# Placing the last two casts and transposes earlier in the list of a fused retention and mixer kernel

## The chip, the cores and the metric

The kernel runs on one core of one Trainium2 chip. The metric is the device time of one execution in microseconds (us). The time before is 333.81 us, the median of three runs (332.57, 333.81 and 334.24). The traced execution is a further one: it took 332.29 us, of which 330.5 us are the span that the profile shows.

The engines are called as in the profile: PE (TensorE, its weight loads apart as PEld), DVE (VectorE), ACT (ScalarE), POOL (GpSimd) and SP (SyncE). Each works through its own list of instructions in order; a `q` behind the name (SPq) is the part that issues DMAs and waits.

## What is computed

Two stages, written as two functions in the reference. The first is a causal retention over 8 batches, 8 heads, 576 positions and a head width of 64; the second is a low-rank mixer over the positions followed by a two-layer block over the channels:

```python
scores = scale * np.matmul(q, k.transpose(0, 1, 3, 2))
Dmat = np.where(rel >= 0, gamma[:, None, None] ** rel[None, :, :], 0.0)   # rel = i - j
attn = np.matmul(scores * Dmat[None], v)
x = attn.transpose(0, 2, 1, 3).reshape(B, S, H * D)        # 8 x 576 x 512
h = x.transpose(0, 2, 1) @ U @ V                           # rank 32 over the positions
u = x + h.transpose(0, 2, 1)
out = u + np.maximum(u @ w_ch1, 0.0) @ w_ch2               # 512 -> 2048 -> 512
```

## The kernel before

**Chunks.** Batches are taken in pairs. The 2 x 576 rows of a pair are nine chunks of 128 rows: chunks 0 to 3 belong to the even batch, chunk 4 is half and half, chunks 5 to 8 belong to the odd one. Over the four pairs that makes 36 chunks, listed in `order` (L542). "Chunk (3, 8)" is chunk 8 of the last pair, pair 3.

**What a chunk needs before PE can use it.** `load` (L219) brings q, k and v as float32 from DRAM into `stage_t` tiles, with DMAs that SP issues. `prep` (L548) then does four things: `cast_qk` casts k to bfloat16 on DVE (L244) and q on ACT (L246), into one tile `qk`; `scale_v` multiplies v by its decay on POOL (L255, tile `vt`); and `xbar` issues one DMA on SP that transposes `qk` into `qkT` (L263). The transpose waits for both casts.

**What uses it.** The attention of a chunk is two items. `A(i)` (L355) runs the score matmuls `SC` on `qkT` (L276) and the matmuls `QS` of q with the running state (L301, which reads `s_sb`), and a mask on DVE (L286). `Bf(i)` (L361) runs `RV` (L315), the scaling `XS` on DVE (L326), and for all but the last chunk of a batch the state update `ST` (L341) with its copy to `s_sb` on ACT (L349). `SJ` is the state update of chunk 4. After a batch's chunks come the mixer items: `MA` (L395), then `MH` and `MT` (L422, L428, L439), which end in the transposed `uT` that the channel block of that batch reads.

**The main work.** The channel block of a batch is 16 `Y1` items (L481, evicted by ACT with a ReLU into `y`, L486) and then 16 `Y2` items of four matmuls each for a batch with four chunks (L515; the sum with u on DVE, L504; the store, L507). Its PSUM tiles come from a pool of three (`ps_big`).

**How the order is made.** The order of instructions is the order of the Python calls. From batch 2 on there is one stretch for each batch b (L1021 to L1030): the main list is the channel block of b, the list `fill` is the attention and the mixer of batch b + 1, and the list `aux` holds preps and loads for chunks later still. `merge` (L16) walks the main list and, before each main item, calls whatever of the other lists has come due. Item k of a list of n falls due at

```python
queues.append([((k + 0.5) / n * lead * total, fn) for k, fn in enumerate(fill)])
```

of the main list's nominal cost, `total`. So `lead` is the share of the stretch at which a list ends: 0.82 for `fill`, 0.58 for `aux`. Where two items fall due before the same main item, `fill` goes first.

**The stretch of batch 6.** Its main list is 32 items of nominal cost 864, total 27648. Its `fill` is `SJ` and the items `A` and `Bf` of chunks 5 to 8 of the last pair, then the mixer: 13 in all. Its `aux` is short: `aux_items` gives a prep for the chunk two places back of each g, and a load only where g is below 36; for batch 6 g runs from 36 to 39, so the list holds two preps, those of chunks (3, 7) and (3, 8), and no loads. For batch 7, g runs from 40 to 44 and the list is empty. The stretches of batches 2 and 4 have the same main list and the same `fill`, with eight `aux` items each, four preps and four loads.

Of the kernel before, what the change touches and what calls it, by code (L numbers as in the profile page):

```python
# [15 lines left out]
def merge(main, *fills, leads=(0.82, 0.64)):  # L16

    total = sum(c for c, _ in main)
    queues = []
    for fill, lead in zip(fills, leads):  # L20
        n = len(fill)
        queues.append([((k + 0.5) / n * lead * total, fn) for k, fn in enumerate(fill)])
    done = 0.0
    for cost, fn in main:
        for q in queues:
            while q and q[0][0] <= done:
                q.pop(0)[1]()
        fn()
        done += cost
    for q in queues:  # L30
        for _, fn in q:
            fn()
# [3 lines left out]
def kernel(  # L36
# [13 lines left out]
    B, H, S, D = q.shape  # L50
# [301 lines left out]
    def attn_items(pr, par):  # L352
        items = []

        def A(i):  # L355
            SC(pr, i)
            if i not in (0, J):
                QS(pr, i)
            mask(pr, i)

        def Bf(i):  # L361
            RV(pr, i)
            if i == J:
                QS(pr, i)
            XS(pr, i)
            if i not in (J, NI - 1):
                ST(pr, i)
                Scopy(pr, i)

        def SJ():  # L370
            ST(pr, J)
            Scopy(pr, J)

        if par == 1:
            items.append(SJ)
        for i in (range(0, J + 1) if par == 0 else range(J + 1, NI)):
            items.append(lambda i=i: A(i))
            items.append(lambda i=i: Bf(i))
        return items
# [86 lines left out]
    def y1_items(par, by_seg=False):  # L466
        nch = 4 + par
        segs = [(0, 4)] if par == 0 else [(0, 3), (3, 2)]
        if by_seg:
            segs = [(1, 4), (0, 1)]  # L470
        items, made = [], []

        def Y1(f, seg):
            if not made:
                made.append(1)
                st["y1", par] = y1_pool.tile(
                    [P, NF, nch * P], BF16, tag=f"y1{par}", name="y1")
            c0, n = segs[seg]
            ps = ps_big.tile([P, 4, P], FP32, tag="big", name="ps_y1")
            for cc in range(NCC):  # L480
                nc.tensor.matmul(  # L481
                    ps[:, 0:n, :], w1_sb[:, cc, f * P:(f + 1) * P],
                    st["uT", par][:, c0:c0 + n, cc, :],
                    start=(cc == 0), stop=(cc == NCC - 1),
                )
            nc.scalar.activation(  # L486
                out=st["y1", par][:, f, c0 * P:(c0 + n) * P],
                in_=ps[:, 0:n, :].rearrange("p s t -> p (s t)"), func=AF.Relu)

        ns = len(segs)  # L490
        for f in range(NF):
            items.append((nch * 216.0, lambda f=f: [Y1(f, g) for g in range(ns)]))
        if by_seg:
            return Y1, items
        return items

    def y2_items(pr, par):
        nch = 4 + par
        items = []

        def store(c, ps, w, last):
            n = w.stop - w.start
            o_sb = osb_pool.tile([P, dm], FP32, tag="o_sb", name="o_sb")
            nc.vector.tensor_tensor(  # L504
                out=o_sb[:, 0:n], in0=ps[:, 0:n], in1=st["u", par][:, c, w], op=ALU.add)
            r0 = pr * 2 * S + (c + (0 if par == 0 else J)) * P
            (nc.sync if last else nc.gpsimd).dma_start(  # L507
                out=out_flat[r0:r0 + P, w], in_=o_sb[:, 0:n])

        def Y2(c, f0):  # L510
            if f0 == 0:
                st["y2"] = ps_big.tile([P, 512], FP32, tag="big", name="ps_y2")
            ps = st["y2"]
            for f in range(f0, f0 + 4):
                nc.tensor.matmul(  # L515
                    ps, st["y1", par][:, f, c * P:(c + 1) * P], w2_sb[:, f, :],
                    start=(f == 0), stop=(f == NF - 1),
                )
            if f0 + 4 == NF:
                store(c, ps, slice(0, dm), pr == B // 2 - 1 and par == 1)  # L520

        def Y2_last(c, w):
            ps = ps_big.tile([P, 512], FP32, tag="big", name="ps_y2")
            n = w.stop - w.start
            for f in range(NF):
                nc.tensor.matmul(  # L526
                    ps[:, 0:n], st["y1", par][:, f, c * P:(c + 1) * P], w2_sb[:, f, w],
                    start=(f == 0), stop=(f == NF - 1),
                )
            store(c, ps, w, True)  # L530

        for c in range(nch):
            if pr == B // 2 - 1 and c == nch - 1 and par == 1:
                for w0, w1 in ((0, 256), (256, 384), (384, 512)):
                    items.append((1728.0, lambda c=c, w=slice(w0, w1): Y2_last(c, w)))
                continue
            for f0 in range(0, NF, 4):
                items.append((864.0, lambda c=c, f0=f0: Y2(c, f0)))
        return items
# [4 lines left out]
    def aux_items(lo, hi):  # L544

        items = []

        def prep(g):  # L548
            pr, i = order[g]
            cast_qk(pr, i)  # L550
            scale_v(pr, i)
            if pr > 0:
                xbar(pr, i)

        for g in range(lo, hi):
            if NI <= g - LAG < len(order):
                items.append(lambda g=g: prep(g - LAG))
            if g < len(order):
                items.append(lambda g=g: load(*order[g], (1, 0, 2)))
        return items  # L560
# [449 lines left out]
    with tc.manual_schedule():  # L1010
        early_consts()
        startup()
        y1_left = first_stretch()
        aux = aux_items(NI + 4, NI + 9)
        aux = [idle] + aux[0:2] + [idle] + aux[2:]
        merge(
            y1_left + y2_items(0, 0) + y2_items(0, 1),
            [idle] + attn_items(1, 0) + mixer_items(1, 0), aux, leads=(0.82, 0.62),
        )
        g = NI + 9  # L1020
        for b in range(2, B):  # L1021
            pr, par = divmod(b, 2)
            fill = []
            if b + 1 < B:
                fill = attn_items((b + 1) // 2, (b + 1) % 2) + mixer_items(
                    (b + 1) // 2, (b + 1) % 2)
            n = 5 if b % 2 == 1 else 4
            aux = aux_items(g, g + n)
            g += n
            merge(y1_items(par) + y2_items(pr, par), fill, aux, leads=(0.82, 0.58))  # L1030

# [1 line left out]
_INS = ['q', 'k', 'v', 'moe_U', 'moe_V', 'moe_w_ch1', 'moe_w_ch2']  # L1033
# [26 lines left out]
```

## Time and profile before

| | us |
|---|---|
| median of three runs | 333.81 |
| the profiled execution | 332.29 |
| its span | 330.5 |
| PE busy | 317.6 (96% of the span) |
| DVE busy | 136.4 (41%) |
| ACT busy | 136.9 (41%) |
| POOL busy | 77.8 (24%) |
| stretch of batch 2 (109.19 to 142.48) | 33.29 |
| stretch of batch 4 (183.01 to 216.30) | 33.29 |
| stretch of batch 6 (256.84 to 292.83) | 35.99 |

The granted TensorE clock is 1.0 throughout. A stretch is taken from its first `Y1` matmul to the first `Y1` matmul of the next batch, on the chain of work that ended last. In the timeline a row is a group of instructions of one line: start, length, engine, line, operation, tiles, count, and in brackets the idle time of the engine before it with what ended it. Lengths of PE rows are modelled and may overlap the next row by some hundredths; start times are records.

### The profile page before, as it was taken

To read this page: it belongs to the slowest core of one execution; us is meant where nothing else is said; L and a number is where in the kernel's file an instruction comes from. 1 tells how busy PE (TensorE), PEld (TensorE's weight loads), DVE (VectorE), ACT (ScalarE), POOL (GpSimd) and SP (SyncE) were. 2 spreads that over 40 slices of the span, in tenths; PEclk is the share of its full clock that TensorE was granted. 3 is DMA by queue.
4 is the path that set the end of the run, shared out by engine and by line. 5 is a ranking of instruction groups with operands and counts; after the bars stand their busy time and mean duration, and the time that the engine had idled before them with its cause. 6 is when DMAs were issued, how large, how long until landed. Compare 5 with 4: busy or idle time off the path is not lost.

```text
span 330.5 us, 7031 instructions
## 1 busy us (share of the span) xinstructions
PE 317.6 (96%) x2942; PEld 174.0 (53%) x2964; DVE 136.4 (41%) x193; ACT 136.9 (41%) x289; POOL 77.8 (24%) x112
## 2 busy tenths in 40 slices
PE   7899999999999999999999999999999996999996
PEld 2464554555444455467644454467644453467544
DVE  5383554444534254534334354534534342510022
ACT  2547656772200573057700573067700662037400
POOL 5675636022221311131121311131211300110000
DMA  7999999999999399949995499959995011330012
GB/s 210 236 226 257 231 196 191 184 171 198 239 238 193 101 226 172 217 125 170 189 251 136 110 218 181 205 135 193 196 211 158 32 34 33 102 106 2 0 70 91
DMA packets 151311, 53.17 MB, mean 161 GB/s; under 512 B 131984, under 2 KB 148752, under 8 KB 151280
## 3 DMA queue, kind: packets, MB, share of 16 engines
q1 hardware_dynamic: 144512, 40.40, 68.0%
q0 software_dynamic: 6768, 12.32, 14.9%
q8 instruction: 23, 0.38, 0.6%
q14 instruction: 8, 0.07, 0.1%
HBM read 36.85 MB, written 9.44 MB: 140 GB/s over the span
## 4 chain that ended last, share of the span: by engine, by line
PE 91%; DMA 3%; DVE 2%; issue 1%; SPq 1%; ACT 1%; POOL 0%
PE ps_y L481 38%; PE ps_y L515 37%; PE psc L276 3%; DMA stage_t<-in_q_dram 2%; PE po L315 2%; PE pss L341 2%; PE pss L691 1%; SPq L578 1%; PE ph L422 1%; PE ps_y L526 1%; PE pa L395 1%; PE po L301 1%; DMA qkT<-qk 1%; DVE xt L682 1%; PE po L665 1%
## 5 line engine op out<-in xcount | busy, mean ns | idle before, releaser
L481 PE MATMUL ps_y<-uT,w_sb 128*128 128x512 bf16 (+3 forms) x768 | 135.8, 326 | 0.4 <-DVE uT L702 0.4
L486 ACT ACTIVATE y<-ps_y 128x384 bf16<-128x384 f32 (+2 forms) x192 | 89.6, 489 | 112.2 <-PE ps_y L481 111.6
L515 PE MATMUL ps_y<-w_sb,y 128*128 128x512 bf16 x538 | 124.5, 379 | 1.5 <-issue 0.8
L481 PEld LDWEIGHTS <-w_sb 128*128 128x128 bf16 x768 | 69.2, 98 | 47.4 <-issue 1.4
L515 PEld LDWEIGHTS <-y 128*128 128x128 bf16 x560 | 52.2, 98 | 59.8
L504 DVE TENSOR_TENSOR o_sb<-ps_y,u 128x512 f32<-128x512 f32 (+2 forms) x38 | 25.2, 663 | 81.5 <-PE ps_y L515 79.3
L255 POOL TENSOR_TENSOR vt<-stage_t,vscale 128x512 bf16<-128x512 f32 (+1 forms) x29 | 30.2, 1049 | 85.2 <-DMA stage_t<-in_v_dram 74.4
L286 DVE TENSOR_TENSOR ret<-psc,tri 128x1024 bf16<-128x1024 f32 x24 | 29.4, 1224 | 44.1 <-PE psc L276 44.1
L507 POOL DMA_DIRECT2D out_dram<-o_sb x31 | 17.2, 554 | 117.5 <-DVE o_sb L504 111.7
L326 DVE TENSOR_TENSOR xt<-po,qscale 128x512 bf16<-128x512 f32 x27 | 18.6, 690 | 25.7 <-PE po L315 24.4
L428 DVE TENSOR_TENSOR u<-ph,xt 128x1024 bf16<-128x1024 f32 (+3 forms) x24 | 21.8, 951 | 11.0 <-PE ph L422 11.0
L246 ACT ACTIVATE qk<-stage_t 128x512 bf16<-128x512 f32 x27 | 16.9, 624 | 8.0 <-DMA stage_t<-in_q_dram 8.0
L401 ACT ACTIVATE a_sb<-pa 128x128 bf16<-128x128 f32 x8 | 2.2, 277 | 34.8 <-PE pa L395 34.8
L349 ACT ACTIVATE s_sb<-pss 128x512 bf16<-128x512 f32 x24 | 14.3, 596 | 4.7 <-PE pss L341 3.6
L647 DVE TENSOR_TENSOR ret<-psc,triU 128x1024 bf16<-128x1024 f32 x8 | 9.7, 1222 | 11.3 <-PE psc L639 11.3
L244 DVE CAST qk<-stage_t 128x512 bf16<-128x512 f32 x27 | 13.1, 485 | 0.9 <-DMA stage_t<-in_k_dram 0.9
L276 PE MATMUL psc<-qkT 64*128 64x128 bf16 x216 | 10.7, 219 | 2.6 <-DMA qkT<-qk 2.6
L596 POOL CAST qk<-stage_t 128x512 bf16<-128x512 f32 x16 | 9.7, 611 | 11.6 <-DMA stage_t<-in_q_dram 8.4
L276 PEld LDWEIGHTS <-qkT 64*128 64x128 bf16 x216 | 6.1, 94 | 11.8 <-issue 8.0
L315 PEld LDWEIGHTS <-ret 128*128 128x128 bf16 x216 | 9.9, 98 | 4.4
L190 PE MATMUL pw<-ident 128*128 128x512 bf16 x33 | 10.2, 448 | 1.4 <-POOL ident masks.py:199 1.4
L315 PE MATMUL po<-vt,ret 128*128 128x64 bf16 x216 | 10.7, 193 | 0.1
(110 smaller groups left out, 159.8 us busy)
## 6 DMA issues: line engine op xcount, KB each, us to landing
stage_t<-in_k_dram SPq DMA_DIRECT2D x32, 256.0 KB, 4.3
stage_t<-in_q_dram SPq DMA_DIRECT2D x32, 256.0 KB, 5.2
stage_t<-in_v_dram SPq DMA_DIRECT2D x32, 256.0 KB, 5.5
out_dram<-o_sb POOLq DMA_DIRECT2D x31, 256.0 KB, 3.4
w_sb<-in_moe_w_ch_dram POOLq DMA_DIRECT2D x4, 512.0 KB, 7.9
w_sb<-in_moe_w_ch_dram POOLq DMA_DIRECT2D x8, 256.0 KB, 9.0
stage_t<-in_k_dram SPq DMA_DIRECT2D x8, 128.0 KB, 3.7
stage_t<-in_q_dram SPq DMA_DIRECT2D x8, 128.0 KB, 4.4
```

The costliest lines, as they stand in the source:

```text
L246: nc.scalar.activation(out=t[rows, 0, :], in_=c["f", 0][rows].rearrange("p h d -> p (h d)"), func=AF.Copy)
L255: (eng or nc.gpsimd).tensor_tensor(out=c["v"][rows], in0=c["f", 2][rows], in1=vscale[rows, i, :, None].to_broadcast([n, H, D]), op=ALU.mult,)
L276: nc.tensor.matmul(psc[:, hl, hp, :], qkT[r, NHP + hp, :], qkT[r, hp, :], start=True, stop=True,)
L286: nc.vector.tensor_tensor(out=ret.rearrange("p (hp hl) i -> p hl hp i", hl=2), in0=c["psc"], in1=m[:, None, None, :].to_broadcast([P, 2, N ...
L315: nc.tensor.matmul(c["po"][:, hl, hp * D:(hp + 1) * D], c["ret"][:, h, :], c["v"][:, h, :], start=(first and hp == 0), stop=True, skip_gro ...
L326: nc.vector.tensor_tensor(out=xt[:, i, :].rearrange("p (hp hl d) -> p hl hp d", hl=2, d=D), in0=c["po"][:, :, 0:NHP * D].rearrange("p hl ( ...
L428: nc.vector.tensor_tensor(out=st["u", par][:, i0 - base:i0 - base + n, w].rearrange("p s (c d) -> p c s d", c=2), in0=ph[k][:, :, 0:n, :], ...
L481: nc.tensor.matmul(ps[:, 0:n, :], w1_sb[:, cc, f * P:(f + 1) * P], st["uT", par][:, c0:c0 + n, cc, :], start=(cc == 0), stop=(cc == NCC - 1),)
L486: nc.scalar.activation(out=st["y1", par][:, f, c0 * P:(c0 + n) * P], in_=ps[:, 0:n, :].rearrange("p s t -> p (s t)"), func=AF.Relu)
L504: nc.vector.tensor_tensor(out=o_sb[:, 0:n], in0=ps[:, 0:n], in1=st["u", par][:, c, w], op=ALU.add)
L507: (nc.sync if last else nc.gpsimd).dma_start(out=out_flat[r0:r0 + P, w], in_=o_sb[:, 0:n])
L515: nc.tensor.matmul(ps, st["y1", par][:, f, c * P:(c + 1) * P], w2_sb[:, f, :], start=(f == 0), stop=(f == NF - 1),)
```

## The change

The second lead of `merge` is 0.58 for batches 2 to 5 as before, and 0.3 for batches 6 and 7:

```diff
-            merge(y1_items(par) + y2_items(pr, par), fill, aux, leads=(0.82, 0.58))
+            merge(y1_items(par) + y2_items(pr, par), fill, aux,
+                  leads=(0.82, 0.58 if b < B - 2 else 0.3))
```

Batch 7's list is empty, so what moves is the two preps in the stretch of batch 6: each is a cast on DVE, a cast on ACT, a multiplication on POOL and a transposing DMA on SP. No instruction is added, removed or changed in shape.

## The prediction

> **What bounds the kernel now.** I read the busy shares first, then the chain that ended last, then that chain in order of time, and last the timeline of the one place where the chain leaves PE. The page's busy line:
>
> ```profile
> PE 317.6 (96%) x2942; PEld 174.0 (53%) x2964; DVE 136.4 (41%) x193; ACT 136.9 (41%) x289; POOL 77.8 (24%) x112
> ```
>
> PE is the bound, and no other engine is near it. So a moved cast or transpose can only matter through a time in which PE stands still. The chain, by engine:
>
> ```profile
> PE 91%; DMA 3%; DVE 2%; issue 1%; SPq 1%; ACT 1%; POOL 0%
> ```
>
> Of the 3% on DMA, 2% is the first load of q. The rest is one wait late in the kernel. The chain in order of time, between 256 and 280 us (start, length, what):
>
> ```profile
> 272.16 0.22 PE pss L341 x4
> 272.39 1.24 PE ps_y L481 x6
> 273.62 3.08 DMA qkT<-qk
> 276.70 0.05 issue
> 276.75 0.40 PE psc L276 x8
> ```
>
> Every earlier step there is PE; here the chain runs through a transposing DMA, and PE resumes when it lands. The timeline says which one:
>
> ```profile
> 263.32 11.54 SPq L263 DMA_TRANSPOSE qkT<-qk  x2
> ...
> 272.20 0.69 DVE L326 TENSOR_TENSOR xt<-po,qscale 128x512 bf16<-128x512 f32 x1 [0.95 <-PE po L315]
> 272.22 1.89 PE L481 MATMUL ps_y<-uT,w_sb 128*128 128x512 bf16 x8
> 272.48 0.60 ACT L349 ACTIVATE s_sb<-pss 128x512 bf16<-128x512 f32 x1
> 272.81 0.42 DVE L244 CAST qk<-stage_t 128x512 bf16<-128x512 f32 x1
> 272.98 0.62 ACT L246 ACTIVATE qk<-stage_t 128x512 bf16<-128x512 f32 x1
> ...
> 276.75 0.40 PE L276 MATMUL psc<-qkT 64*128 64x128 bf16 x8 [2.64 <-DMA qkT<-qk]
> ```
>
> This is chunk (3, 8). Its casts end at 272.98 + 0.62 = 273.60, the transpose starts at 273.62 and its landing frees the score matmuls at 276.75. PE had finished the matmuls before them at 272.22 + 1.89 = 274.11. It is PE's only wait for a transpose in the trace. Last, busy time by stretch, of batch 4 and of batch 6:
>
> ```profile
> 183.01:216.30 33.29, 33.02 (x283) 16.01 (x284) 15.11 (x20) 13.61 (x25) 6.33 (x8) 1.00 0.94 179
> 256.84:292.83 35.99, 33.09 (x283) 16.00 (x284) 14.11 (x18) 12.65 (x23) 4.25 (x6) 1.00 0.26 63
> ```
>
> The columns are the stretch, its length, busy time and count of PE, PEld, DVE, ACT and POOL, the granted clock, the DMA share and GB/s. Both have the same PE work (283 records, 284 weight loads), yet the second is 2.70 us longer, though its DMA engines are busy 26% of the time instead of 94%.
>
> **The change part by part.** *Where the two preps go.* An item of cost 864 in a total of 27648. Before, they fell due at 0.25 x 0.58 = 0.145 and 0.435 of it, 4009 and 12026, so before main items 5 and 14 (counted from 0). After: 0.075 and 0.225, 2074 and 6221, so before items 3 and 8. The score matmuls of chunk (3, 7) fall due at 5.5/13 x 0.82 (item 12), those of chunk (3, 8) at 7.5/13 x 0.82 (item 16). The margin ahead of the latter grows from 2 main items to 8; ahead of the former from 7 to 9.
>
> *The stall that goes.* Where no transpose is late, the start of eight Y1 matmuls and that of the score matmuls behind them lie 267.76 to 269.58 = 1.82 us apart (chunk 7 of this stretch). For chunk (3, 8) they lie 272.22 to 276.75 = 4.53 apart: 2.71 too much. The stretches say the same, 35.99 - 33.29 = 2.70. That is the term: -2.70 us, if the transpose lands before 272.22 + 1.82 = 274.04.
>
> *When it lands now.* On DVE the cast of k moves ahead of xt of chunk 6, the mask and xt of chunk 7, to just behind the mask of chunk 6. That mask runs 265.56 to 266.78, the cast 0.42, to 267.20. On ACT the cast of q moves ahead of six evictions and two copies to s_sb, to behind the eviction that starts at 265.22: it runs 265.82 to 266.44. So SP issues at about 267.2. The landing time at the new place is not in the trace; the bounds are 3.1 us (both transposes of this stretch) and 12.5 us (the longest of all 27, before 110 us, where nearly all DMA slices are full). I take 3.1, the row nearest in place and load: 270.3, 3.7 us ahead of need. Even 4.5, the longest in the stretch of batch 5, with loads beside it, leaves 2.3.
>
> *What the moved casts cost.* DVE, chunk 8: the cast fits the 0.95 us that DVE idles before xt of chunk 6 (267.74). Without that cover xt would start at most 0.42 late. DVE, chunk 7: the cast moves ahead of the mask of chunk 5, into an idle time of 3.53 us before 261.10. It waits only for loads: SP issued the last at 242.66 and landings in that window took at most 6.1 us, so all are in by about 250. Behind it wait the mask and then PE's matmuls on `ret`; a cast there could be felt only if it ended after 261.10. ACT, chunk 8: 0.62 us into the 0.82 idle before the eviction at 266.64. ACT, chunk 7: two evictions earlier, directly behind the one that ends at 260.50; it delays the next by 261.12 - 260.76 = 0.36, to an end at 261.72. With three PSUM tiles, PE writes that tile again from 263.30, so 1.6 us of cover remain. From both sides: 0 to +0.62 us, a whole cast, should that cover fail; I take 0. POOL and SP: the two multiplications and two transposes keep their places in those lists, with nothing between to be moved past; POOL has already run ahead of PE and done both by 260.47. PE's list is the same, instruction for instruction. What leaves the old places (casts at 272.81 and 272.98) was cover for nothing else.
>
> [...] The trace has three casts of k that ran beside POOL's multiplication, and they took longer: at 194.52, 232.68 and 238.03 us, 0.75, 0.72 and 1.13 us instead of 0.42, each ending 0.3 us after POOL's. The moved cast of chunk 7 goes to about 257.56, next to POOL's pair (258.42 to 260.47). [...]
>
> *What is late next.* At 274.04 the score matmuls need the PSUM tile that the mask of chunk 7 frees (270.02 + 1.23 = 271.25), and the matmuls behind them need xt of chunk 7 done (272.89) and s_sb (272.48 + 0.60 = 273.08). The latest clears with about 1 us, and ACT has one cast less before it. After the score matmuls all work follows PE, so it shifts by the same amount; the stretch of batch 4 runs through the same order with no wait.
>
> *Sum.* -2.70 + 0. The profiled execution took 332.29 us (span 330.5, 1.8 around it): 329.59, span 327.8. The median shown is 1.52 above the profiled execution, so the prediction for a median is 333.81 - 2.70 = 331.1 us.
>
> **The rivals.**
>
> *The transposes land late (slower).* One mechanism: the DMA for chunk (3, 8), issued at 267.2, meets other transfers. Up to 6.8 us to land it costs nothing; from 9.55 us on (276.75) it is a loss; at the trace's longest, 12.5, PE resumes at 279.7, 2.95 us later than now: 336.8. For it: such a landing exists. Against: it was in a full stretch; here no loads remain, and both transposes took 3.1. A landing of 8 us would leave a gain of 2.70 - 1.16 = 1.54 us, 332.3.
>
> *The wait moves (smaller gain).* A cast on ACT or DVE pushes an eviction or a mask that PE waits for, in the first third of the stretch. Worst, from the rows: 0.62 for each cast of q and 0.42 for each cast of k, 2.08 if nothing covers any: a gain of 0.62, 333.2. For it: the moved ACT cast of chunk 7 does delay an eviction, by 0.36. Against: the covers above, and the stretch of batch 4, which holds four such preps among the same work in 33.29.
>
> *The stall was hidden or particular to the profiled execution (no change).* 333.8. For it: the profiled execution is the shortest of the four, so the others lose time that this trace does not show. Against: the stall follows from the order alone, cast, transpose, score matmuls two items apart, and the 2.70 us reappears on PE as the difference of whole stretches. That the list does not move far enough is excluded by the item counts.
>
> **How the numbers follow.** 0.5% of 333.81 is 1.67 us, about what a measurement of this kernel tells from no change. The forecast holds 0.84, the smaller gain 0.06, no change 0.06, late landing 0.04. Forecast times: from 332.57 - 2.70 = 329.9 to 334.24 - 2.70 = 331.5 by the runs shown, and 329.6 by the profiled one. I reach a little lower, 329.4, and upward to the 8 us landing's 332.3, which takes in an uncovered cast (331.1 + 0.62 = 331.7). The forecast can measure under 0.5% by scatter alone, so: faster 0.86, same 0.10, slower 0.04.
>
> **What would show it right or wrong.** Right: no idle before the score matmuls of L276 in the stretch of batch 6; its length 33.3; both transposes issued near 261.1 and 267.2; casts of 0.42 and 0.62 at 257.6, 266.8 (DVE) and 260.5, 265.8 (ACT). Wrong: idle time on PE before L276, L315 or L481 in 257 to 277, released by DVE, ACT or the transpose; or a stretch that shrank while a later one grew.

## The result, and the profile after

The changed kernel takes 329.52 us, the median of four runs (329.26 to 331.06), against 333.31 us for the kernel before (332.57 to 334.24, four runs). The ratio is 0.9895, with a 95% interval of 0.9853 to 0.9937: faster by 1.05%, and the interval excludes no change. The prediction was 331.1 us, in a range of 329.4 to 332.3, with 0.86 for faster. The profiled execution after takes 329.63 us with a span of 327.8; the profiled one before took 332.29 with 330.5. From profile to profile that is 2.66 us, as forecast; from median to median it is 3.79. The missing 1.1 us is the one thing that the prediction did not see, and the experiments trace most of it.

The chain of work that ended last, in order of time, for the changed kernel (start, length, what), at the place where it ran through a transpose before:

```profile
272.17 0.22 PE pss L341 x4
272.40 1.73 PE ps_y L481 x8
274.12 0.33 PE psc L276 x8
274.45 0.12 PE po L301 x8
274.57 1.83 PE ps_y L515 x8
```

The chain no longer leaves PE. The timeline of the same kernel gives the casts and transposes their new places:

```profile
257.49 0.42 DVE L244 CAST qk<-stage_t 128x512 bf16<-128x512 f32 x1
...
258.43 2.05 POOL L255 TENSOR_TENSOR vt<-stage_t,vscale 128x512 bf16<-128x512 f32 x2
...
260.40 0.62 ACT L246 ACTIVATE qk<-stage_t 128x512 bf16<-128x512 f32 x1
...
260.92 0.59 ACT L486 ACTIVATE y<-ps_y 128x512 bf16<-128x512 f32 x1
261.05 7.46 SPq L263 DMA_TRANSPOSE qkT<-qk  x2
...
265.73 0.62 ACT L246 ACTIVATE qk<-stage_t 128x512 bf16<-128x512 f32 x1
...
266.71 0.42 DVE L244 CAST qk<-stage_t 128x512 bf16<-128x512 f32 x1
...
274.06 0.40 PE L276 MATMUL psc<-qkT 64*128 64x128 bf16 x8
```

The casts of chunk (3, 8) end at 267.13 and its transpose starts at 261.05 + 7.46 - 1.23 = 267.28 (1.23 is the issue time of one on SP). It lands 3.1 us later, at 270.4, and the score matmuls start at 274.06 with no idle time in brackets: 3.7 us to spare. Busy time by stretch, batch 4 and batch 6 (length, then busy time and count of PE, PEld, DVE, ACT, POOL, then clock, DMA share, GB/s):

```profile
183.01:216.30 33.29, 33.29 (x286) 15.99 (x284) 15.29 (x20) 13.60 (x25) 6.34 (x8) 1.00 0.95 179
256.84:290.12 33.28, 33.28 (x286) 16.00 (x284) 14.12 (x18) 12.79 (x23) 4.25 (x6) 1.00 0.28 68
```

The stretch of batch 6 has the length of that of batch 4; it was 35.99. Between 60 and 320 us PE now waits for nothing that the profile names (before: 2.6 us for the transpose).

### The profile page after: what moved, and what is told of

Read it like the earlier page. It is cut to its first block, busy times and chain, and to the rows that moved or that the text cites. A ratio compares the mean times of both kernels' runs of the same rounds, so it can differ in the third digit from the quotient of the medians.

```text
span 327.8 us, 7053 instructions
## 1 busy us (share of the span) xinstructions
PE 319.5 (97%) x2964; PEld 174.1 (53%) x2964; DVE 137.1 (42%) x193; ACT 137.0 (42%) x289; POOL 78.4 (24%) x112
## 4 chain that ended last, share of the span: by engine, by line
PE 88%; DMA 5%; SPq 3%; DVE 1%; issue 1%; POOL 0%; ACT 0%
PE ps_y L515 38%; PE ps_y L481 38%; DMA stage_t<-in_q_dram 3%; PE psc L276 3%; DMA stage_t<-in_v_dram 2%; SPq L578 2%; PE po L315 2%; PE pss L341 2%; PE ph L422 1%; PE ps_y L526 1%; PE po L301 1%; PE pa L395 1%; DVE xt L682 1%; PE pss L691 1%; PE psc L639 0%
## 5 line engine op out<-in xcount | busy, mean ns | idle before, releaser
L515 PE MATMUL ps_y<-w_sb,y 128*128 128x512 bf16 x560 | 127.0, 380 | 0.0
L515 PEld LDWEIGHTS <-y 128*128 128x128 bf16 x560 | 52.2, 98 | 59.9
L244 DVE CAST qk<-stage_t 128x512 bf16<-128x512 f32 x27 | 14.8, 548 | 0.0
L315 PEld LDWEIGHTS <-ret 128*128 128x128 bf16 x216 | 9.9, 98 | 4.4
L315 PE MATMUL po<-vt,ret 128*128 128x64 bf16 x216 | 10.7, 193 | 0.0
```

The costliest lines, as they stand in the source:

```text
L315: nc.tensor.matmul(c["po"][:, hl, hp * D:(hp + 1) * D], c["ret"][:, h, :], c["v"][:, h, :], start=(first and hp == 0), stop=True, skip_gro ...
L515: nc.tensor.matmul(ps, st["y1", par][:, f, c * P:(c + 1) * P], w2_sb[:, f, :], start=(f == 0), stop=(f == NF - 1),)
```

## The experiments

Below, "the length of the stretch" is the time from the first `Y1` matmul of batch 6 to the first of batch 7, by their start times in the timeline: 36.00 us before (256.67 to 292.67), 33.29 after (256.68 to 289.97). "The wait" is PE's idle time before the score matmuls of chunk (3, 8). "The clock" is the mean granted TensorE clock of a whole execution. The start-up shifts whole timelines against each other by about a microsecond (batch 6 starts between 255.69 and 256.82), so expected and measured moments are compared by their distances.

**First theory:** PE waits only for the transpose of chunk (3, 8), which follows the later of its two casts; the place of those casts is the whole change.

**1. Only the prep of chunk (3, 8) moved.** A list of one item falls due at half its lead, so each prep gets a list of its own:

```diff
-            merge(y1_items(par) + y2_items(pr, par), fill, aux,
-                  leads=(0.82, 0.58 if b < B - 2 else 0.3))
+            main = y1_items(par) + y2_items(pr, par)
+            if b == B - 2:
+                merge(main, fill, aux[0:1], aux[1:2], leads=(0.82, 0.29, 0.45))
+            else:
+                merge(main, fill, aux, leads=(0.82, 0.58))
```

> Only the prep of chunk (3, 8) is placed as in the changed kernel; that of chunk (3, 7) stays where it was before. Theory (PE waits for nothing but the transpose of chunk (3, 8), which lands 3.1 us after the later of its two casts): casts end near 267.1, the transpose lands near 270.4, the stretch of batch 6 takes 33.28 us as in the changed kernel, the profiled execution 329.6. Rival (part of the gain comes from the earlier prep of chunk (3, 7)): a stretch between 33.3 and 36.0, so that the two halves add up to the 2.7.

Measured: stretch 33.29, no wait; 328.93 us against 332.45 for the kernel before beside it, ratio 0.9896 (0.9851 to 0.9941). The whole gain of the change is in this one prep.

**2. Only the prep of chunk (3, 7) moved.**

```diff
-                merge(main, fill, aux[0:1], aux[1:2], leads=(0.82, 0.29, 0.45))
+                merge(main, fill, aux[0:1], aux[1:2], leads=(0.82, 0.15, 0.87))
```

> Only the prep of chunk (3, 7) is moved; that of chunk (3, 8) stays late. Theory: nothing is gained, the transpose of chunk (3, 8) starts at 273.6, lands at 276.7, the stretch takes 36.0 us and the profiled execution 332.3. Rival (both preps share in the gain): a stretch clearly below 36.0.

Measured: the transpose of chunk (3, 8) starts at 273.49, and PE waits 2.68 us, as before. But the stretch takes 37.70 us (256.54 to 294.24), not 36.0, and the execution 333.87. Nothing is gained, as both the theory's order of events and the wait say; yet 1.7 us are lost that no wait explains. The timeline of PE in this kernel, after the wait:

```profile
276.66 0.40 PE L276 MATMUL psc<-qkT 64*128 64x128 bf16 x8 [2.68 <-DMA qkT<-qk]
276.89 0.28 PE L301 MATMUL po<-s_sb,qkT 64*128 64x64 bf16 x8
277.33 2.53 PE L515 MATMUL ps_y<-w_sb,y 128*128 128x512 bf16 x7 [0.16 <-issue]
279.65 0.64 PE L315 MATMUL po<-vt,ret 128*128 128x64 bf16 x8
280.10 2.53 PE L515 MATMUL ps_y<-w_sb,y 128*128 128x512 bf16 x8
282.56 0.46 PE L395 MATMUL pa<-xt,U_O 128*32 128x128 bf16 x20
282.96 1.90 PE L515 MATMUL ps_y<-w_sb,y 128*128 128x512 bf16 x7
```

The matmuls of L315 take 0.64 us here and 0.40 in the changed kernel, and eight of L515 take 2.53 instead of 1.9; by 283 us both are as usual. The windows of this kernel, with the columns as above; the granted clock is the third number from the end:

```profile
276.66:278.00 1.34, 1.18 (x20) 0.82 (x22) 0.90 (x1) 0.00 (x0) 0.00 (x0) 1.00 0.00 0
278.00:279.00 1.00, 1.00 (x4) 0.41 (x3) 0.32 (x1) 0.00 (x0) 0.00 (x0) 0.50 0.00 0
279.00:280.00 1.00, 1.00 (x10) 0.49 (x8) 0.00 (x0) 0.00 (x0) 0.00 (x0) 0.50 0.00 0
280.00:281.00 1.00, 1.00 (x9) 0.45 (x7) 0.67 (x1) 0.00 (x0) 0.00 (x0) 0.50 0.00 0
281.00:282.00 1.00, 1.00 (x5) 0.41 (x4) 0.02 (x1) 0.00 (x0) 0.00 (x0) 0.80 0.00 0
282.00:283.00 1.00, 1.00 (x24) 0.43 (x23) 0.33 (x1) 0.00 (x0) 0.00 (x0) 1.00 0.07 16
```

After the wait the clock is 0.50 for some 3.4 us. From the score matmuls to the next batch's first `Y1` it is 276.66 to 294.24 = 17.58 us here; in the profile of the kernel before it was 276.75 to 292.67 = 15.92. (The trace of that execution holds no clock record; that its clock stayed up is read from these 15.92 us, which are those of the changed kernel, 274.06 to 289.97.) So 1.66 us go to the clock.

**3. The prep of chunk (3, 8) half way, lead 0.5.** That of chunk (3, 7) then stands before main item 4, between its old place (5) and its new one (3).

```diff
-                  leads=(0.82, 0.58 if b < B - 2 else 0.3))
+                  leads=(0.82, 0.58 if b < B - 2 else 0.5))
```

> The lead of the list is 0.5 in place of 0.3, so the prep of chunk (3, 8) stands before main item 12, between the old place (14) and the new one (8). Theory: its cast on DVE follows the mask of chunk 7 and ends at 271.65, the transpose lands 3.1 us later at 274.75, PE needs it at 274.06 and waits 0.7 us; stretch 33.28 + 0.7 = 34.0, profiled execution 330.3. Rival (a threshold: any earlier place removes the wait whole): 33.3. Rival (the place on the list counts, not the time of the casts: two of the six main items give a third of the gain): 35.1.

Measured: stretch 34.72 (256.19 to 290.91), wait 1.36 us, execution 330.56. The wait follows the end of the casts, without a threshold and not by the place on the list, but it is twice as long as expected: the transpose started at 271.25, 0.15 us after its cast on DVE had ended, and took 3.70 us to land instead of 3.1. The expected 0.7 used a landing time that was too short by 0.6; a second execution of the same kernel (number 9) also took 3.7. In both, the DMA view of 270 to 276 us shows one transfer on the instruction queue beside the transpose, which the changed kernel does not show between 266 and 272. In the profile of number 1 the transpose of chunk (3, 7) took 4.8 us, in that of number 10 about 4.9 (the two have a median of 4.0, and that of chunk (3, 8) took 3.1), and their DMA views have a transfer on the instruction queue too (261 to 270 us in number 1, 255 to 278 in number 10). But so have those of numbers 2, 6 and 8 between 255 and 278 us, where both transposes landed in 3.1; and in the kernel before such a transfer started at 265.87, 0.04 us before the transpose's last packet ended, and the landing took 3.1. In the changed kernel and in numbers 4 and 7 both landed in 3.1 as well. That the one delays the other was not tried by an edit.

**4. The prep of chunk (3, 8) one main item later, lead 0.62.** The edit is that of number 3, with 0.62.

> The lead is 0.62, so the prep of chunk (3, 8) stands one main item later than before the change. On DVE nothing moves; on ACT the cast of q falls behind one more eviction, which starts at 273.30. Theory: that cast runs 273.8 to 274.4, the transpose lands at 277.55, PE waits 3.5 us instead of 2.7; stretch 36.8, profiled execution 333.1, slower than the kernel before by 0.8. Rival (DVE's cast or the transposing queue sets the wait): unchanged, 36.0.

Measured: the cast of q runs 273.93 to 274.55 on ACT, the transpose starts at 274.57, PE waits 3.43 us. That is the theory's wait, and the rival is out: DVE's cast did not move. The stretch is 38.45 us (256.82 to 295.27), not 36.8, the execution 334.89. Again 17.58 us lie between the score matmuls and the next batch, and again 1.66 of them are the clock's.

**5. Other transfers beside the transposes.** The changed lead, and nine loads that nothing reads:

```diff
+                def extra(i):
+                    for j in (1, 0, 2):
+                        t = stage.tile([P, H, D], FP32, tag="stage", name="stage_t")
+                        nc.sync.dma_start(
+                            out=t, in_=(q, k, v)[j][B - 2, :, i * P:(i + 1) * P, :].rearrange(
+                                "h s d -> s h d"))
+
+                aux = [lambda: extra(0), aux[0], lambda: extra(1), lambda: extra(2), aux[1]]
```

> The changed lead, with nine more loads of 256 KB (three chunks of q, k and v of batch 6, into tiles that nothing reads) issued around the two transposes, which puts transfers beside them as in the stretches of batches 2 and 4. Theory: the transpose of chunk (3, 8) is issued near 267.9 and lands 3.2 to 4.5 us later, before 274.06, so PE does not wait and the stretch stays at 33.3. Rival (the transposes land late among other transfers, up to 12.5 us): landing near 280, a wait of up to 6 us, stretch up to 39, slower than the kernel before.

Measured: stretch 33.29, execution 328.89, no wait for the transpose. The DMA share of the stretch rose from 0.28 to 0.66. The landings took 3.2 and 4.2 us, as in the stretches with loads (3.2 to 4.3 us in those of batches 2 and 4 of the kernel before). What came close to deciding was something else. From the timeline of this kernel:

```profile
266.50 0.62 ACT L246 ACTIVATE qk<-stage_t 128x512 bf16<-128x512 f32 x1
267.80 1.02 SPq L1036 DMA_DIRECT2D stage_t<-in_v_dram  x1
268.99 2.01 SPq L263 DMA_TRANSPOSE qkT<-qk  x1
273.41 0.40 PE L276 MATMUL psc<-qkT 64*128 64x128 bf16 x8
```

The casts end at 267.12, but SP is still issuing loads ahead of the transpose and starts it at 268.99, 1.9 us late; with 4.2 us to land it is there by 273.2, some 0.2 us before PE needs it. (L1036 is the line of the added loads.) The rival of late landing is not seen; a delay in SP's list, which the prediction had excluded only because nothing stood between, takes up half of the spare time.

**6. The casts early, the call for the transpose at its old place.**

```diff
+                casts = lambda: (cast_qk(3, 8), scale_v(3, 8))
+                merge(main, fill, aux[0:1], [casts], [lambda: xbar(3, 8)],
+                      leads=(0.82, 0.15, 0.45, 0.87))
```

> The casts of chunk (3, 8) are placed as in the changed kernel, but the call that issues its transpose stays at its old place in the list. Theory (SP has nothing between, and starts the transpose when the later cast is done): transpose at 267.3, no wait on PE, stretch 33.3, as if the whole prep had moved. Rival (the place of the DMA's call sets its time): transpose at 273.6, stretch 36.0.

Measured: transpose at 266.28, stretch 33.29, no wait, 328.63 us. Where the DMA is called in the list does not matter here; the casts release it.

**7. Only the cast of q early.** The cast on ACT gets the place of the changed kernel; the cast on DVE, the multiplication and the transpose stay:

```diff
+                merge(main, fill, aux[0:1], [cast_q], [rest], leads=(0.82, 0.15, 0.45, 0.87))
```

> Of chunk (3, 8) only the cast of q on ACT is placed as in the changed kernel; the cast of k on DVE, the multiplication and the transpose stay at the old place. Theory (the transpose waits for the later of two casts): the cast of k ends at 273.23, the transpose starts at 273.25 and lands at 276.35, a gain of 0.37 only, stretch 35.6. Rival (ACT's queue was the cause, DVE's cast was free to run earlier): stretch 33.3.

Measured: the cast of k runs 271.97 to 272.39, the transpose starts at 272.53, the wait is 2.43 us, the stretch 35.79 (255.83 to 291.62), 331.24 us. Measured from the start of the stretch the cast of k ended when expected, but SP starts the transpose 0.14 us after a cast on DVE (0.15 in the changed kernel) and 0.02 after one on ACT, as in the kernel before. So the gain is 0.2 us where 0.37 was expected. The two casts must move together.

**8. The changed kernel again, five rounds.** No edit.

> The changed kernel once more, timed in five rounds against the kernel before. Theory (a wait of 2.7 us is gone and nothing else): ratio 1 - 2.7/333.3 = 0.992, and all waits of PE before the first load of weights for batch 2 as in the kernel before. Rival (there is a further gain of about 1 us, as the medians 333.31 and 329.52 suggest): ratio 0.989 or below, with spans that differ by more than 2.7 us.

Measured: 329.12 us (328.69 to 329.65, six executions) against 332.26 (330.91 to 333.82, eleven), ratio 0.9901 (0.9868 to 0.9933). The interval holds both 0.992 and 0.989, so by itself it decides nothing. The other part of the expectation failed: PE's waits in the first 60 us, which sum to 5.2 us in the profile of the kernel before, sum to 4.3 here, so the start-up alone scatters by almost a microsecond. Sorting the executions by their clock says more. Of the eleven of the kernel before, five have a clock of 0.999 or 1.0 and a mean of 331.55 us, six have 0.993 to 0.995 and a mean of 333.23. All six of the changed kernel have 0.999 or 1.0. The difference of the two means, 1.68 us, is close to the 1.66 of number 2. Where in these executions the clock fell no trace shows; a mean of 0.995 over 332 us is what 3.4 us at half clock give. An execution whose trace has no clock record reads 1.0 too (the profiled ones of the kernel before and of number 5 do), so the counts of falls below may be too low. One execution of the changed kernel, the 331.06 us of the result, is 1.4 us longer than the next and reads 1.0; why is not known.

**Second theory:** the wait has a second price. When PE stands idle for about 2.6 us, the clock afterwards falls to one half for some 3.4 us, but only in part of the executions. **Its rival:** the clock falls by itself.

**9. The shorter wait, five rounds.** The kernel of number 3 again.

> The kernel with lead 0.5, whose wait is 1.4 us, in five rounds beside the kernel before, whose wait is 2.6. Second theory (the wait has a second price: after a wait of that length the granted clock of TensorE falls to about one half for some 3.4 us in part of the executions, which costs 1.66 us more; the mean clock of the execution then reads 0.993 to 0.995 instead of 0.999 or 1.0): at 1.4 us the clock seldom or never falls, at most one execution in six below 0.998, all times within 1 us of each other. Rival (the clock falls by itself, without regard to this wait): about half of the executions below 0.998, as with the kernel before.

Measured: none of six executions below 0.999; 330.59 us (330.1 to 331.83, so a spread of 1.7 us, wider than expected), ratio 0.9936 (0.991 to 0.9961).

**10. The wait kept, but filled.** The order of the kernel before, with matmuls that nothing reads ahead of chunk (3, 8):

```diff
+            if b == B - 2:
+                a8 = fill[7]
+
+                def filled():
+                    ps = ps_big.tile([P, 4, P], FP32, tag="big", name="pfill")
+                    for _ in range(8):
+                        nc.tensor.matmul(
+                            ps, ident, ident[:, None, :].to_broadcast([P, 4, P]),
+                            start=True, stop=True)
+                    a8()
+
+                fill[7] = filled
             merge(y1_items(par) + y2_items(pr, par), fill, aux, leads=(0.82, 0.58))
```

> The order of the kernel before, with the wait kept, but eight matmuls of 128x512 on a constant, some 1.8 us that nothing reads, put in front of the score matmuls of chunk (3, 8), so that PE works through most of the wait. Second theory (what lowers the clock is PE standing idle): the transpose still lands near 276.7, the wait still costs 2.7 us, but no execution reads below 0.998; span as the kernel before has it without the fall, so a time about 0.8 us below its mean. Rival (the clock falls for another reason): about half of the executions below 0.998 and no gain.

The timeline of PE in this kernel, from the last `Y1` matmuls to the score matmuls of chunk (3, 8):

```profile
271.67 1.89 PE L481 MATMUL ps_y<-uT,w_sb 128*128 128x512 bf16 x8
273.40 1.89 PE L1036 MATMUL pfill<-ident 128*128 128x512 bf16 x8
276.20 0.40 PE L276 MATMUL psc<-qkT 64*128 64x128 bf16 x8 [0.92 <-DMA qkT<-qk]
```

Measured: the stretch is 36.00 us (256.12 to 292.12), the same as before, so the 2.7 us are still lost. (L1036 is the line of the added matmuls.) Yet none of twelve executions is below 0.999, and the time is 331.64 us (331.03 to 332.2), ratio 0.9963 (0.9945 to 0.998) to the kernel before, 12 of whose 23 executions beside it are below 0.998. The rival, that the clock falls for another reason than PE standing idle, is out. Work that computes nothing makes the kernel 0.4% faster. Of the 1.2 us between the means (332.86 and 331.65), 0.7 are the clock's, the distance of all 23 executions from the eleven at full clock (332.13). The other 0.5 is not explained; the stretch did not shrink, and it is no more than the start-up scatters.

**11. The longer wait, five rounds.** The kernel of number 4 again.

> The kernel with lead 0.62, whose wait is 3.4 us, in five rounds. Second theory (the longer PE stands idle, the more executions lose clock): at least four executions in six below 0.998, and those 1.7 us longer than the others; median about 1.5 us above the median of the kernel before. Rival (the clock falls by itself): half of the executions, median 0.8 above.

Measured: 8 of 12 executions at 0.995 or below, with a mean of 334.75 us, the other four with 332.51: 2.2 us apart, more than the 1.7 expected. Four of the eight read 0.990, and the profile is of one of them: its clock is 0.50 from about 276.0 us, before the wait ends at 277.15, until about 282.8, some 6.8 us in all, and 18.60 us (277.15 to 295.75) lie between the score matmuls and the next batch. Its windows, with the columns as above:

```profile
275.00:276.00 1.00, 0.00 (x0) 0.00 (x0) 0.00 (x0) 0.00 (x0) 0.00 (x0) 0.98 0.85 165
276.00:277.00 1.00, 0.00 (x0) 0.00 (x0) 0.00 (x0) 0.00 (x0) 0.00 (x0) 0.50 0.52 97
282.00:283.00 1.00, 1.00 (x4) 0.40 (x3) 0.66 (x1) 0.00 (x0) 0.00 (x0) 0.61 0.00 0
```

The median is 334.34, 1.56 above the kernel before; ratio 1.0032 (1.0005 to 1.0059).

| kernel | wait of PE before chunk (3, 8), us | executions below 0.998 |
|---|---|---|
| changed kernel (here and in number 8), numbers 1, 5, 6 | none | 0 of 16 |
| filled (10) | 0.9 | 0 of 12 |
| lead 0.5 (3 and 9) | 1.4 | 0 of 7 |
| kernel before, the executions beside numbers 1, 8, and 9 to 11 | 2.6 (profile) | 21 of 41 |
| only the cast of q early (7) | 2.4 | 0 of 1 |
| only chunk (3, 7) moved (2) | 2.7 | 1 of 1 |
| lead 0.62 (4 and 11) | 3.4 | 9 of 13 |

## Why the prediction was right, and what it missed

*The stall that goes* was right: the wait of 2.64 us is gone and the stretch is 2.71 shorter, against 2.70 forecast. Numbers 1, 2 and 6 show that the casts of chunk (3, 8) alone carry it.

*When it lands now* was right to a tenth: casts to end at 267.2 (267.13), issue at 267.2 (267.28), landing after 3.1. The bound of 4.5 with loads beside held in number 5 (4.2), but a landing of 4.8 without loads was seen in the profile of number 1; here it would still have left 2 us.

*What the moved casts cost* was right at nothing. The cast of chunk 7 on ACT delayed the next eviction, to an end at 261.51 (forecast 261.72), and PE did not notice. The cast of chunk 7 on DVE took 0.42 us and ended at 257.91, before POOL started at 258.43, so how long a cast beside POOL's multiplication takes did not matter. The count of such long casts was short: the trace of the kernel before has five, those at 67.22 and 120.70 us (0.68 and 0.63) too, each ending 0.3 us after POOL's.

*What is late next* was right: nothing. s_sb was done at 273.09 for 274.06.

*The rivals.* Late landing was not seen, in number 5 either. The wait did not move. "Hidden or particular to the profiled execution" fell, but the sentence under it, that the profiled execution is the shortest of the four and the others lose time that the trace does not show, was the clue to what was missed.

*The sum* is the step that was mis-sized. It took the profile's 2.70 us as the whole gain and set it off from a median whose executions were not all like the profiled one. The profile of the kernel before caught an execution at full clock. In 21 of 41 executions the mean clock says that the half clock followed, at a price of 1.66 us. The term is thus -2.70 in every execution and another -1.66 in about half, -2.70 - 0.51 x 1.66 = -3.55 in the mean, an estimate from these numbers; measured were 3.79 and 3.14 from median to median (here and in number 8). By executions at full clock alone, the mean of the kernel before lies 331.55 - 329.15 = 2.40 above the changed kernel in number 8, and 332.06 - 329.05 = 3.01 above the kernel of number 1: scatter around 2.70. That is also most of why 329.52 came out 1.6 us below the forecast. That it still lies in the range, 0.1 us above the low end, is luck: 329.4 was set a little under the profiled execution's 329.6, with no thought of the clock.

## What to carry to other kernels

A transposing DMA is a step like any other: count back from its reader through the landing and the later of its inputs' casts, and compare stretches that run the same work to find the one that waits. A wait of the bounding engine can cost more than its length, here 1.66 us more in half of the executions, and a single trace may show an execution in which it did not; compare the mean clock of several executions before taking a profile's wait as the whole price. If a wait can't be removed, filling it with matmuls that nothing reads can be worth a part of it, 0.4% here (number 10).

## What the runs showed of the hardware that was not expected

In three profiles the granted clock fell to 0.50 after a long wait of TensorE: for 3.4 us after 2.68 (number 2) and 3.43 us (number 4), for 6.8 us after 3.46 (number 11). By the mean clock it fell in 21 of 41 executions with a wait of 2.6 us, in 9 of 13 with 3.4, and in none of 19 with 0.9 or 1.4. In number 2 the fall came 1.3 us after PE had resumed, in the profile of number 11 while it still stood idle.

The length of the wait alone does not decide it. A fall followed the wait of 2.68 us in number 2 and none that of 2.43 in number 7 (one execution each), and with one and the same list of instructions the kernel before fell in about half of its executions. Nor does the fall come at one distance from the wait: by the windows it came at 278.00, 278.76 and 275.96 us in numbers 2, 4 and 11, which is 4.0, 4.5 and 2.3 us after PE's idle time had begun. What makes the clock fall in one execution and not in the next is not shown: no experiment moved a wait of one length, and the only trace of the kernel before holds no clock record.
